# The last output feature of a two-dimensional Fourier stage: a third matmul per slice in every batch, in place of a path of its own

## The chip, the cores and the metric

The kernel runs on one core of one Trainium2 chip. The metric is the device time of one execution, in microseconds (us). A core has a matrix engine (PE, with PEld for the loading of its stationary operand), a vector engine (DVE), a scalar engine (ACT), a general engine (POOL) and a queue engine (SP) that here only issues DMA transfers. Each engine takes its instructions in the order of its own queue; they meet through semaphores.

## The reference

The input x is 8 batches of 3072 positions by 256 features. What is computed is the real part of a Fourier transform over positions and features, and on that a channel mix with a shift by one position:

```
X  = fft(fft(x, axis=1), axis=2).real
xk = mu_k * X + (1 - mu_k) * X_prev      # X_prev: one position earlier, 0 at the first
xr = mu_r * X + (1 - mu_r) * X_prev
k  = relu(xk @ w_k);  v = (k * k) @ w_v  # w_k 256x1024, w_v 1024x256
r  = sigmoid(xr @ w_r)                   # w_r 256x256
out = r * v                              # 8 x 3072 x 256, float32
```

## The kernel before

**The Fourier part of a batch.** Positions are 48 x 64. Stage A (a_item, line 391; a_sum, line 403, for inputs that have not been through the butterfly) transforms over the 48, with the weights w_pm. Stage D (d_item, line 426) transforms over features, with the table w_eo, into g_all: 24 units of 386 columns on 128 partitions, of which columns 1 to 256 hold values and the others zeros. Stage C (c_item, line 437) transforms over the 64, with the tables m1 and m2. It makes 27 slices of 64 columns, in items of 7, 7, 7 and 6 slices (in batch 0: 5, 4, 8, 8 and 2). For a slice it takes 128 columns of a unit of g_all as the stationary operand and 64 columns of a table as the moving one: columns 128 to 255 with m1 into one half of a PSUM tile, columns 0 to 127 with m2 into the other half. The ACT engine copies both halves to pq; `halves` (line 477) makes the sum and the difference of them in y, `diff` (line 484) the difference of neighbouring positions in d, and `mix` (line 518) the inputs of the channel mix.

**Feature 128.** The values of feature 128 stand in column 256 of a unit, outside the two blocks of 128 columns, and must be brought into row 0 of the second half. In batch 0 a third matmul does this: columns 256 to 383 (one column of values, 127 of zeros) with m1, added to the same PSUM columns as the second. In batches 1 to 7 it goes another way. `turned` (line 461, three DVE instructions) multiplies column 256 of all units by the table tw into u; after the last slice of the batch two matmuls with 27 columns of u as stationary operand and the table cs as moving one make a 27x64 block (line 454) in spare columns of the same PSUM tile; an ACT instruction copies it to f (line 459); `flat` (line 469) clears one element of f on DVE and sends f by a DMA on the SP queue into row 0 of y. Columns 63 and 127 of w_eo differ between the two ways: `eo_rest` (line 364) sets them for the first, and `plain_128` (line 370) changes them for the second, once, in step 5. The tables cs and tw are cut from m1 and m2 in `m_rest(0)` (line 296, instructions at lines 302 to 305 and 318) and in `plain_128` (line 376).

**The order of the work.** Up to line 629 the order is that of the code: stages A, D and C of batch 0 while the tables are still being made, with filler matmuls on zeros (keep_busy, line 138). From line 731 on there are 192 + 5 steps, 24 to a batch. Each step does one quarter of the product with w_k for a chunk of 512 positions (k_piece, line 541), then the items of matmuls that the table `work` has for this step (kind "x": stages A, D, C and the product with w_r), then a quarter of the product with w_v of five steps before (v_tile, line 566), then the DVE items of the step (kind "w"), then the output (v_out, line 577) and in odd steps the square (line 550). So stages A, D and C of a later batch stand between the products of an earlier one. `pin_order` (line 85) holds every engine to the order in which the code issues. PSUM is three tiles of 1024 columns, in turn (psW), and two of 512 (psV).

The lines of c_item that decide between the two ways:

```
for o, col, m, first, last in ((0, 128, m1, True, True), (512, 0, m2, True, b > 0),
                               (512, 256, m1, False, True))[:2 if b else 3]:
...
if b and s0 + n == NSL:
    for k in range(2):
        nc.tensor.matmul(out=ps[0:NSL, 448:512], lhsT=y_t[b, "u"][:, k],
                         rhs=cs[:, k], start=(k == 0), stop=(k == 1))
```

Of the kernel before, what the change touches and what calls it, by code (L numbers as in the profile page):

```python
# [10 lines left out]
FP16 = mybir.dt.float16  # L11
INT32 = mybir.dt.int32
UINT32 = mybir.dt.uint32
AF = mybir.ActivationFunctionType
ALU = mybir.AluOpType
# [5 lines left out]
def _v(ap, extra_offset, free_dims):  # L21
    new_ap = [list(ap.ap[0])] + [[s, c] for (s, c) in free_dims]
    return dataclasses.replace(ap, offset=ap.offset + extra_offset, ap=new_ap)
# [12 lines left out]
def kernel(  # L36
# [10 lines left out]
    nc = tc.nc  # L47
# [3 lines left out]
    P = 128  # L51
    N1, R = 48, 64
    NSL = 27
    GU = 386
    NS1 = 9

    const = ctx.enter_context(tc.tile_pool(name="const", bufs=1))
    xh_pool = ctx.enter_context(tc.tile_pool(name="xh", bufs=2))
    eo_pool = ctx.enter_context(tc.tile_pool(name="eo", bufs=2))
    y_pool = ctx.enter_context(tc.tile_pool(name="y_sb", bufs=1))  # L60
# [13 lines left out]
    def ps_w():  # L74
        return ps_slot("W", 3, 1024)
# [37 lines left out]
    V = nc.vector  # L113
# [54 lines left out]
    def phase(lo, hi):  # L168
        lo, hi = (lo + 0.5) % 1.0, (hi + 0.5) % 1.0
        if (lo, hi) not in phs:  # L170
            t = const.tile([P, 1], FP32, name=f"ph{len(phs)}")
            V.memset(t[0:64], lo * TURN)
            V.memset(t[64:128], hi * TURN)
            phs[lo, hi] = t
        return phs[lo, hi]
# [5 lines left out]
    g_all = const.tile([P, NU, GU], FP16)  # L181

    def g_zeros(u0, u1):
# [25 lines left out]
                    op0=ALU.mult, op1=ALU.add)  # L209
# [3 lines left out]
                    scalar2=1.0 / N1, op0=ALU.mult, op1=ALU.mult)  # L213
    V.tensor_tensor(out=u48, in0=u48, in1=ph48.rearrange("p a b -> p (a b)"), op=ALU.add)
    V.tensor_scalar(out=r48, in0=u48, scalar1=MAGIC, scalar2=MAGIC,
                    op0=ALU.add, op1=ALU.subtract)
# [3 lines left out]
    for g in range(2):  # L220
        for n in range(2):
            V.tensor_scalar(out=w_sg[:, n, g:g + 1], in0=hi48, scalar1=2.0 * g - 1.0,
                            scalar2=1.0 - g, op0=ALU.mult, op1=ALU.add)
        V.tensor_scalar(out=w_sg[:, 2, g:g + 1], in0=hi48, scalar1=1.0 - 2.0 * g,
                        scalar2=g - 1.0, op0=ALU.mult, op1=ALU.add)
# [5 lines left out]
                    op0=ALU.bitwise_and, op1=ALU.logical_shift_right)  # L231
    V.tensor_tensor(out=w_pm, in0=_v(t48, 0, [(0, 3), (1, 48), (0, 2)]),
                    in1=_v(w_sg, 0, [(2, 3), (0, 48), (1, 2)]), op=ALU.mult)
    V.tensor_scalar(out=pos_l, in0=pcol_i, scalar1=1, scalar2=5,
                    op0=ALU.bitwise_and, op1=ALU.logical_shift_left)
# [7 lines left out]
                    scalar2=float(TURN) / R, op0=ALU.mult, op1=ALU.mult)  # L243
# [3 lines left out]
                    scalar2=phase(0.25, 0.0), op0=ALU.mult, op1=ALU.add)  # L247
# [21 lines left out]
    m1 = const.tile([P, NSL, 64], FP16)  # L269
    m2 = const.tile([P, NSL, 64], FP16)  # L270


    tw = const.tile([P, 2, NSL], FP16)
    cs = const.tile([P, 2, 64], FP16)

    def m_angles(s0, s1):
        V.tensor_tensor(out=ang[:, s0:s1], in0=_v(ast, s0, [(1, s1 - s0), (0, 64)]),
                        in1=_v(ast, NSL, [(0, s1 - s0), (1, 64)]), op=ALU.add)
# [9 lines left out]
    lo64, hi64 = slice(0, 64), slice(64, 128)  # L288
# [7 lines left out]
    def m_rest(part):  # L296

        s = 26 if part else 0  # L300
        if not part:
            V.tensor_copy(out=cs[lo64, 0], in_=m1[lo64, 1])
            V.tensor_copy(out=cs[hi64, 0], in_=m2[hi64, 1])
            V.tensor_copy(out=cs[hi64, 1], in_=m1[hi64, 1])
            V.tensor_scalar(out=cs[lo64, 1], in0=m2[lo64, 1], scalar1=-1.0, scalar2=None,
                            op0=ALU.mult)
        if part:
            V.tensor_scalar(out=m2[hi64, 25], in0=m1[hi64, 25], scalar1=-1.0, scalar2=None,
                            op0=ALU.mult)
            V.tensor_copy(out=m1[hi64, 25], in_=m1[lo64, 25])  # L310
        for m in (m1, m2):
            V.tensor_scalar(out=m[hi64, s], in0=m[hi64, s], scalar1=-1.0, scalar2=None,
                            op0=ALU.mult)
            if part:
                V.memset(m[lo64, 25], 0.0)
            else:
                V.memset(m[hi64, 1], 0.0)
                V.tensor_copy(out=tw[:, 0 if m is m1 else 1, 0:1], in_=m[:, 0, 0:1])
                V.memset(m[:, 0, 0:1], 0.0)

    m_angles(0, NS1)
# [3 lines left out]
    w_eo = const.tile([P, 2, 128], FP16)  # L325
    V.tensor_scalar(out=pd_f, in0=pcol_f, scalar1=float(TURN) / D, scalar2=None, op0=ALU.mult)
    for c in range(2):
        V.tensor_scalar(out=ueo[:, :, c], in0=veo_i[:, :, c], scalar1=pd_f,
                        scalar2=(0.5 + 0.25 * c) * TURN, op0=ALU.mult, op1=ALU.add)
# [34 lines left out]
    def eo_rest():  # L364

        for col, sign in ((63, 0.5), (127, -0.5)):
            V.tensor_scalar(out=w_eo[:, 0, col:col + 1], in0=w_eo[:, 0, 127:128], scalar1=sign,
                            scalar2=0.5, op0=ALU.mult, op1=ALU.add)

    def plain_128():  # L370

        V.memset(w_eo[:, 0, 63:64], 1.0)
        V.tensor_scalar(out=w_eo[:, 0, 127:128], in0=w_eo[:, 0, 127:128], scalar1=-2.0,
                        scalar2=1.0, op0=ALU.mult, op1=ALU.add)
        for n, m in enumerate((m1, m2)):
            V.tensor_copy(out=tw[:, n, 1:NSL], in_=m[:, 1:NSL, 0])


    a_t = {}
    y_t = {}  # L380
# [56 lines left out]
    def c_item(b, s0, n, eng="A"):  # L437

        if s0 == 0:
            y_t[b] = y_pool.tile([P, 2, NSL, 64], FP16, name="y")  # L440
            y_t[b, "pq"] = y_pool.tile([P, 2, NSL, 64], FP16, name="pq")
        pq = y_t[b, "pq"]
        ps = ps_w()
        for i in range(n):
            sl = s0 + i
            u = {-1: 1, 24: 0, 25: 23}.get(sl - 1, sl - 1)
            for o, col, m, first, last in ((0, 128, m1, True, True), (512, 0, m2, True, b > 0),
                                           (512, 256, m1, False, True))[:2 if b else 3]:
                nc.tensor.matmul(out=ps[:, o + 64 * i:o + 64 * i + 64],  # L449
                                 lhsT=g_all[:, u, col:col + 128], rhs=m[:, sl],  # L450
                                 start=first, stop=last)
        if b and s0 + n == NSL:
            for k in range(2):
                nc.tensor.matmul(out=ps[0:NSL, 448:512], lhsT=y_t[b, "u"][:, k],
                                 rhs=cs[:, k], start=(k == 0), stop=(k == 1))
        evac(pq[:, :, s0:s0 + n, :], _v(ps, 0, [(512, 2), (64, n), (1, 64)]), eng)
        if b and s0 + n == NSL:
            y_t[b, "f"] = f = y_pool.tile([NSL, 64], FP16, name="f")
            nc.scalar.activation(out=f, in_=ps[0:NSL, 448:512], func=AF.Copy)

    def turned(b):

        y_t[b, "u"] = u = y_pool.tile([P, 2, NSL], FP16, name="u")
        for s0, n, u0, step in ((1, 24, 0, 1), (25, 2, 0, 23), (0, 1, 1, 1)):
            V.tensor_tensor(out=u[:, :, s0:s0 + n],
                            in0=_v(g_all, GU * u0 + 256, [(0, 2), (GU * step, n)]),
                            in1=tw[:, :, s0:s0 + n], op=ALU.mult)

    def flat(b):

        V.memset(y_t[b, "f"][0:1, 0:1], 0.0)
        nc.sync.dma_start(out=y_t[b][0:1, 1], in_=y_t[b, "f"])


    x_t = {}
# [159 lines left out]
    def at(step, f, *args):  # L635
        work.setdefault((step, "x" if f in (a_item, a_sum, d_item, c_item, r_item) else "w"),
                        []).append((f, args))
# [48 lines left out]
    at(14, mix, 0, 1, 1, 1)  # L686
    for n, st0 in enumerate((7, 8, 9, 10)):
        at(st0, a_item, 1, 1, n // 2, n % 2, "A")
    at(5, plain_128)
    for n, st0 in enumerate((12, 13, 13, 14, 15, 17)):  # L690
        at(st0, d_item, 1, n)
    at(18, turned, 1)
    for n, st0 in enumerate((14, 15, 18, 19)):
        at(st0, c_item, 1, (0, 7, 14, 21)[n], 7 if n < 3 else 6)

    for b in range(B):
        s0 = 24 * b

        for n, st0 in enumerate((2, 4, 6, 8) if b else ()):
            at(s0 + st0, mix, b, n // 2, 1, n % 2)  # L700
        if b + 3 < B:
            for h in range(2):
                at(s0 + 12 + 2 * h, load_xh, b + 3, h)
        t = b + 2
        if t < B:
            for n, st0 in enumerate((9, 10, 12, 14) if b else (11, 13, 15, 24)):
                at(s0 + st0, butterfly, t, n // 2, n % 2)
            for n, st0 in enumerate((18, 19, 21, 22, 23, 25, 26, 27)):
                at(s0 + st0, a_item, t, n // 4, n // 2 % 2, n % 2)
            for n, st0 in enumerate((29, 30, 31, 34, 35, 38)):  # L710
                at(s0 + st0, d_item, t, n)
            at(s0 + 39, turned, t)
            for n, st0 in enumerate((33, 37, 39, 41)):
                at(s0 + st0, c_item, t, (0, 7, 14, 21)[n], 7 if n < 3 else 6)
        t = b + 1
        if t < B:
            at(s0 + 16, halves, t, 0, 14)
            at(s0 + (18 if b else 20), halves, t, 14, 27)
            at(s0 + (19 if b else 20), diff, t, 0, 26, (0,))
            at(s0 + (18 if b else 20), flat, t)  # L720
            at(s0 + (20 if b else 22), diff, t, 0, 26, (1,))
            at(s0 + 21, mix, t, 0, 0, 0)
            at(s0 + 22, mix, t, 0, 0, 1)
            at(s0 + 24, mix, t, 1, 0, 0)
            at(s0 + 25, mix, t, 1, 0, 1)
# [51 lines left out]
```

## Time and profile before

| what | value |
|---|---|
| three runs | 461.36, 461.0 and 460.77 us; median 461.0 us |
| the profiled execution | 461.36 us; span from its first to its last instruction 459.5 us |
| PE busy | 450.2 us, 98% of the span |
| PEld, DVE, ACT, POOL busy | 329.2, 361.6, 357.9, 34.9 us |
| mean granted clock of PE | 0.998 |

The span is counted from the first instruction; the remaining 1.9 us of the execution lie around it. A timeline gives, for each engine, the start of a run of instructions, its length, line and count, and in brackets the idle time before it and what ended it. Matmuls are pipelined, so neighbouring entries on PE overlap: a matmul of 64 columns is shown with some 193 ns, but what it costs the engine is the distance from its start to the start of the next. "psW<-m,g_all" is a matmul that writes psW from m and g_all. Line 386 and line 384 are the helper that copies out of PSUM on ACT and on DVE.

### The profile page before, as it was taken

To read this page: it belongs to the slowest core of one execution; us is meant where nothing else is said; L and a number is where in the kernel's file an instruction comes from. 1 tells how busy PE (TensorE), PEld (TensorE's weight loads), DVE (VectorE), ACT (ScalarE), POOL (GpSimd) and SP (SyncE) were. 2 spreads that over 40 slices of the span, in tenths; PEclk is the share of its full clock that TensorE was granted. 3 is DMA by queue.
4 is the path that set the end of the run, shared out by engine and by line. 5 is a ranking of instruction groups with operands and counts; after the bars stand their busy time and mean duration, and the time that the engine had idled before them with its cause. 6 is when DMAs were issued, how large, how long until landed. Compare 5 with 4: busy or idle time off the path is not lost.

```text
span 459.5 us, 9810 instructions
## 1 busy us (share of the span) xinstructions
PE 450.2 (98%) x4089; PEld 329.2 (72%) x4089; DVE 361.6 (79%) x533; ACT 357.9 (78%) x397; POOL 34.9 (8%) x67
## 2 busy tenths in 40 slices
PE   8889999999999999999999999999999999999996
PEld 4657777777777777777777777777777777676765
DVE  7899978987788777978688777888679855898443
ACT  3898898788878887888878888878887888666662
POOL 8821000001000000000000000000000000000000
PEclk9999999999999999999999999999999999999999
DMA  7995462625623373324722265222222232323324
GB/s 120 147 170 100 110 137 47 139 66 119 139 47 71 56 150 95 70 58 91 165 56 65 52 138 118 69 51 66 58 60 61 56 70 47 71 59 80 70 66 95
DMA packets 32972, 40.25 MB, mean 88 GB/s; under 512 B 4480, under 2 KB 30592, under 8 KB 31584
## 3 DMA queue, kind: packets, MB, share of 16 engines
q1 hardware_dynamic: 28080, 25.07, 22.8%
q0 software_dynamic: 4688, 14.42, 18.6%
q8 instruction: 32, 0.52, 0.5%
q10 hardware_dynamic: 160, 0.13, 0.1%
q14 instruction: 12, 0.10, 0.1%
HBM read 28.84 MB, written 25.17 MB: 118 GB/s over the span
## 4 chain that ended last, share of the span: by engine, by line
PE 92%; DVE 4%; DMA 2%; issue 1%; ACT 0%; POOL 0%; SPq 0%; DVEq 0%; POOLq 0%
PE psV L573 36%; PE psW L536 35%; PE psW L559 9%; PE psW L422 4%; PE psW L398 4%; PE psW L449 3%; PE psW L412 1%; DMA xh<-in_x_dram 1%; DVE t L501 1%; DVE x L514 1%; DMA out_dram<-o 1%; DVE y L481 0%; DVE d L489 0%; DVE a L384 0%; DVE pq L384 0%
## 5 line engine op out<-in xcount | busy, mean ns | idle before, releaser
L546 ACT ACTIVATE rl<-psW 128x1024 f16<-128x1024 f32 x192 | 196.7, 1025 | 83.6 <-PE psW L536 83.6
L536 PE MATMUL psW<-x,wk 128*128 128x512 f16 (+1 forms) x776 | 197.4, 377 | 1.6 <-DVE x L514 1.3
L573 PE MATMUL psV<-wv_sb,k 128*128 128x256 f16 x1536 | 198.7, 273 | 0.0
L552 DVE TENSOR_TENSOR k<-rl 128x2048 f16<-128x2048 f16 x96 | 117.4, 1223 | 62.5 <-ACT rl L546 61.9
L573 PEld LDWEIGHTS <-k 128*128 128x128 f16 x1536 | 143.6, 98 | 20.6
L536 PEld LDWEIGHTS <-wk 128*128 128x128 f16 x776 | 75.7, 98 | 52.4 <-issue 3.1
L582 DVE SCALAR_TENSOR_TENSOR o<-psV,r 128x512 f32<-128x512 f32 (+1 forms) x97 | 66.3, 684 | 24.9 <-PE psV L573 22.4
L514 DVE TENSOR_TENSOR x<-y,t 128x1536 f16<-128x1536 f16 (+2 forms) x74 | 63.0, 851 | 2.5
L386 ACT ACTIVATE a<-psW 128x768 f16<-128x768 f32 x62 | 49.8, 807 | 4.4 <-PE psW L412 4.2
L559 PE MATMUL psW<-wr,x 128*128 128x256 f16 x384 | 49.8, 273 | 0.0
L564 ACT ACTIVATE r<-psW 128x1024 f16<-128x1024 f32 x48 | 49.0, 1021 | 0.8 <-PE psW L559 0.8
L559 PEld LDWEIGHTS <-x 128*128 128x128 f16 x384 | 37.6, 98 | 14.4 <-issue 0.2
L386 ACT ACTIVATE g_all<-psW 128x1024 f16<-128x1024 f32 (+1 forms) x47 | 47.8, 1024 | 0.0
L106 POOL DMA_DIRECT2D xh<-in_x_dram x38 | 20.0, 533 | 239.0 <-DVE eo L119 223.5
L422 PEld LDWEIGHTS <-a 128*128 128x128 f16 x384 | 25.0, 98 | 11.1 <-DVE a L384 1.0
L398 PEld LDWEIGHTS <-eo 96*128 96x128 f16 x416 | 23.4, 97 | 11.6
L119 DVE TENSOR_TENSOR eo<-xh 96x2048 f16<-96x2048 f16 x26 | 31.5, 1213 | 0.0
L422 PE MATMUL psW<-w_eo,a 128*128 128x128 f16 x376 | 28.3, 219 | 0.3 <-ACT pq L386 0.3
L386 ACT ACTIVATE pq<-psW 128x896 f16<-128x896 f32 (+5 forms) x32 | 27.6, 865 | 0.3 <-PE psW L449 0.3
L398 PE MATMUL psW<-w_pm,eo 96*128 96x96 f16 x416 | 26.3, 206 | 0.0
L449 PEld LDWEIGHTS <-g_all 128*128 128x128 f16 x459 | 17.8, 98 | 7.0 <-ACT g_all L386 0.2
L501 DVE TENSOR_SCALAR t<-d,mu_f 128x1536 f16<-128x1536 f16 (+2 forms) x42 | 22.5, 535 | 0.2
(103 smaller groups left out, 155.8 us busy)
## 6 DMA issues: line engine op xcount, KB each, us to landing
out_dram<-o SPq DMA_DIRECT2D x190, 128.0 KB, 2.4
xh<-in_x_dram POOLq DMA_DIRECT2D x28, 384.0 KB, 6.1
xh<-in_x_dram POOLq DMA_DIRECT2D x6, 192.0 KB, 6.4
wv_sb<-in_moe_w_v_dram POOLq DMA_DIRECT2D x1, 512.0 KB, 8.8
xh<-in_x_dram POOLq DMA_DIRECT2D x4, 96.0 KB, 6.9
out_dram<-o ACTq DMA_DIRECT2D x2, 64.0 KB
out_dram<-o SPq DMA_DIRECT2D x2, 64.0 KB
y<-f SPq DMA_DIRECT2D x7, 3.4 KB
```

What stands on the lines that cost most here:

```text
L386: nc.scalar.activation(out=out_ap, in_=in_ap, func=AF.Copy)
L398: nc.tensor.matmul(out=ps[:, 128 * i:128 * i + 96], lhsT=eo[:, 8 * j + i, e, :], rhs=w_pm[0:96, 0], start=True, stop=True)
L422: nc.tensor.matmul(out=_v(ps, 256 * i + 64 * (1 - e), [(128, 2), (1, 64)]), lhsT=a_t[b][:, e, 2 * u:2 * u + 2, :], rhs=w_eo[:, e, :], star ...
L449: nc.tensor.matmul(out=ps[:, o + 64 * i:o + 64 * i + 64], lhsT=g_all[:, u, col:col + 128], rhs=m[:, sl], start=first, stop=last)
L514: V.tensor_tensor(out=dst, in0=_v(y_t[b], 64 * (NSL * a + lo + 3 * m), [(1, n)]), in1=_v(x_t["t", a], 64 * lo, [(1, n)]), op=ALU.subtract ...
L536: nc.tensor.matmul(out=st["k", ds][:, 512 * hs + lo:512 * hs + hi], lhsT=wk_sb[m][a][:, 128 * fc:128 * fc + 128], rhs=xk[:, a, 512 * i + l ...
L546: nc.scalar.activation(out=st["rl"][:, 2 * ds:2 * ds + 2], in_=st["k", ds].rearrange("p (f t) -> p f t", f=2), func=AF.Relu, bias=0.0, sca ...
L552: V.tensor_tensor(out=k2_t[c][:, 2 * ds - 2:2 * ds + 2], in0=r, in1=r, op=ALU.mult)
L559: nc.tensor.matmul(out=ps[:, 256 * tb:256 * tb + 256], lhsT=x_t[b, 1, m][:, a, 512 * i + 128 * tb: 512 * i + 128 * tb + 128], rhs=wr_sb[m] ...
L564: nc.scalar.activation(out=st["r", c], in_=ps, func=AF.Sigmoid)
L573: nc.tensor.matmul(out=st["v"][:, 256 * h:256 * h + 256], lhsT=k2_t[c][:, fc, 128 * tb:128 * tb + 128], rhs=wv_sb[:, fc], start=(fc == 0), ...
L582: V.scalar_tensor_tensor(out=o.rearrange("p a b -> p (a b)")[:, 0:256 * n], in0=st["v"][:, 0:256 * n], scalar=16.0, in1=st["r", c][:, 256 ...
```

## The change

The path of its own for feature 128 goes, and all batches take the way of batch 0: a third matmul per slice. With it go the tables tw and cs and the instructions that fill them, `plain_128`, `turned`, `flat`, the two matmuls per batch and the copy to f. One DVE instruction of batch 1, the second half of `diff`, stands in step 21 in place of step 22.

```diff
-    tw = const.tile([P, 2, NSL], FP16)
-    cs = const.tile([P, 2, 64], FP16)
...
         s = 26 if part else 0
-        if not part:
-            V.tensor_copy(out=cs[lo64, 0], in_=m1[lo64, 1])
-            V.tensor_copy(out=cs[hi64, 0], in_=m2[hi64, 1])
-            V.tensor_copy(out=cs[hi64, 1], in_=m1[hi64, 1])
-            V.tensor_scalar(out=cs[lo64, 1], in0=m2[lo64, 1], scalar1=-1.0, scalar2=None,
-                            op0=ALU.mult)
...
                 V.memset(m[hi64, 1], 0.0)
-                V.tensor_copy(out=tw[:, 0 if m is m1 else 1, 0:1], in_=m[:, 0, 0:1])
                 V.memset(m[:, 0, 0:1], 0.0)
...
-    def plain_128():
-
-        V.memset(w_eo[:, 0, 63:64], 1.0)
-        V.tensor_scalar(out=w_eo[:, 0, 127:128], in0=w_eo[:, 0, 127:128], scalar1=-2.0,
-                        scalar2=1.0, op0=ALU.mult, op1=ALU.add)
-        for n, m in enumerate((m1, m2)):
-            V.tensor_copy(out=tw[:, n, 1:NSL], in_=m[:, 1:NSL, 0])
...
-            for o, col, m, first, last in ((0, 128, m1, True, True), (512, 0, m2, True, b > 0),
-                                           (512, 256, m1, False, True))[:2 if b else 3]:
+            for o, col, m, first, last in ((0, 128, m1, True, True), (512, 0, m2, True, False),
+                                           (512, 256, m1, False, True)):
...
-        if b and s0 + n == NSL:
-            for k in range(2):
-                nc.tensor.matmul(out=ps[0:NSL, 448:512], lhsT=y_t[b, "u"][:, k],
-                                 rhs=cs[:, k], start=(k == 0), stop=(k == 1))
         evac(pq[:, :, s0:s0 + n, :], _v(ps, 0, [(512, 2), (64, n), (1, 64)]), eng)
-        if b and s0 + n == NSL:
-            y_t[b, "f"] = f = y_pool.tile([NSL, 64], FP16, name="f")
-            nc.scalar.activation(out=f, in_=ps[0:NSL, 448:512], func=AF.Copy)
-
-    def turned(b):
...
-    def flat(b):
...
-    at(5, plain_128)
...
-    at(18, turned, 1)
...
-            at(s0 + 39, turned, t)
...
-            at(s0 + (18 if b else 20), flat, t)
-            at(s0 + (20 if b else 22), diff, t, 0, 26, (1,))
+            at(s0 + (20 if b else 21), diff, t, 0, 26, (1,))
```

More of the change, by code (lines that the diff above doesn't have):

```diff
@@ L451, in c_item @@
                                  start=first, stop=last)
-        if b and s0 + n == NSL:
-            for k in range(2):
-                nc.tensor.matmul(out=ps[0:NSL, 448:512], lhsT=y_t[b, "u"][:, k],
-                                 rhs=cs[:, k], start=(k == 0), stop=(k == 1))
         evac(pq[:, :, s0:s0 + n, :], _v(ps, 0, [(512, 2), (64, n), (1, 64)]), eng)
-        if b and s0 + n == NSL:
-            y_t[b, "f"] = f = y_pool.tile([NSL, 64], FP16, name="f")
-            nc.scalar.activation(out=f, in_=ps[0:NSL, 448:512], func=AF.Copy)
-    def turned(b):
[L463 to L467, printed above, removed]
-    def flat(b):
-        V.memset(y_t[b, "f"][0:1, 0:1], 0.0)
-        nc.sync.dma_start(out=y_t[b][0:1, 1], in_=y_t[b, "f"])
     x_t = {}
```

## The prediction

> **What bounds the kernel now.** I read the page's busy times and its chain first. PE is busy for 98% of the span and makes 92% of the chain that ended last; DVE makes 4%.
>
> ```profile
> PE 450.2 (98%) x4089; PEld 329.2 (72%) x4089; DVE 361.6 (79%) x533; ACT 357.9 (78%) x397; POOL 34.9 (8%) x67
> ...
> PE 92%; DVE 4%; DMA 2%; issue 1%; ACT 0%; POOL 0%; SPq 0%; DVEq 0%; POOLq 0%
> ```
>
> A share is an average, so I asked for the waits between 36 and 451 us and for busy times by stretches of one batch (54.2 us).
>
> ```profile
> ACT rl L546 <- PE psW L536: 82.8, 182, 0.7
> DVE k L552 <- ACT rl L546: 61.9, 64, 1.2
> ...
> ```
>
> ```profile
> 109.20:163.40 54.20, 54.20 (x507) 40.00 (x505) 43.30 (x54) 44.43 (x50) 2.01 (x4) 1.00 0.41 89
> ```
>
> The answer on the waits has seven rows, and in none of them does PE wait; ACT waits for PE 182 times, DVE for ACT. In the stretch, after its length, PE is busy 54.20 of 54.20 us, DVE 43.30, ACT 44.43, at a granted clock of 1.00. So from 36 us to the last products PE alone sets the pace: each nanosecond put into or taken out of its queue is one of the time, and DVE and ACT have 10 us per batch to spare. Before 34 us it is otherwise; there the chain runs over DVE.
>
> **Stage C in batches 1 to 7.** A busy matmul overlaps the next, so I take distances from start to start in the timeline of PE.
>
> ```profile
> 164.32 0.57 PE L449 MATMUL psW<-m,g_all 128*128 128x64 f16 x14
> 164.73 1.04 PE L573 MATMUL psV<-wv_sb,k 128*128 128x256 f16 x8
> ...
> 173.40 0.51 PE L449 MATMUL psW<-m,g_all 128*128 128x64 f16 x12
> 173.85 0.23 PE L454 MATMUL psW<-cs,u 128*27 128x64 f16 x2
> 174.01 1.05 PE L573 MATMUL psV<-wv_sb,k 128*128 128x256 f16 x8
> ```
>
> ```profile
> 30.28 0.86 PE L449 MATMUL psW<-m,g_all 128*128 128x64 f16 x24
> 30.97 1.03 PE L536 MATMUL psW<-x,wk 128*128 128x512 f16 x4
> ```
>
> An item of 7 slices has 14 matmuls and lasts 0.41 us (to the nanosecond, the start times say 407): 29.1 ns for a weight load and a matmul. The batch-0 item of 8 slices shows the very form that the change brings to the others, three matmuls per slice, the third adding to what the second wrote: 24 in 0.69 us, 29 ns again. The last item of a batch has 12 matmuls, which should take 12 x 29.1 = 0.35 us, but the pair of line 454 starts 0.444 us after them and lasts 0.165: the item takes 0.609 us, and the pair costs 0.26 us, not 0.06.
>
> Per batch, before: 3 x 0.407 + 0.609 = 1.83 us. After: 27 slices x 3 = 81 matmuls x 29.1 ns = 2.36 us. Difference 0.53 us; seven batches: **+3.69 us**.
>
> A rule speaks for a dearer change here. The Trainium skill, page "TensorE: Matmul & The Clock Gate", section "LDWEIGHTS (loading the stationary operand)", makes the load time proportional to the columns loaded, so that the 27-column pair would be no dearer than two common matmuls. With the pair at 2 x 29.1 ns, the change would cost 7 x 25 x 29.1 ns = 5.1 us here; the trace shows 0.26 us for the pair, and I go by it. The same page, section "Back-to-back issue gap", gives about 81 ns for a sustained pair of load and matmul at 128 columns; at that price for each of the 27 added, less the pair, the sum would be 7 x (27 x 0.081 - 0.26) = 13.5 us. The trace shows 29 ns at 64 columns.
>
> **What goes from DVE, ACT and SP in those batches.** Per batch: three DVE instructions of `turned` (0.238, 0.156 and 0.163 us) and one of 0.059, an ACT copy of 0.201 us and one DMA issue of 0.78 us on SP. All of it lies under PE, which waits for none of it, and nobody waits for f by the trace: worth 0. Were DVE the pace, it would be 0.62 us per batch. `plain_128` (0.34 us of DVE at 38.1 us) lies after PE's last start-up wait, which ends at 33.14: 0. The half of `diff` that moves up a step (1.02 us) passes one `mix` on DVE. Behind it then stand the rest of that step's `mix`, a square and an output. The next product that needs this work starts at 79.52 us, 0.1 us after the second `mix` ends; but what DVE does before that instant is the same in sum, less the 0.62 us above, so it is no later: 0. The moved step issues no DMA.
>
> **The start-up.** Here six DVE instructions go from the chain.
>
> ```profile
> 11.85 0.17 DVE L302 COPY cs<-m 64x64 f16<-64x64 f16 x1
> 12.03 0.18 DVE L303 COPY cs<-m 64x64 f16<-64x64 f16 x1
> 12.13 0.18 DVE L304 COPY cs<-m 64x64 f16<-64x64 f16 x1
> 12.33 0.17 DVE L305 TENSOR_SCALAR cs<-m 64x64 f16<-64x64 f16 x1
> ...
> 13.02 0.16 DVE L318 COPY tw<-m 128x1 f16<-128x1 f16 x1
> ...
> 13.56 0.16 DVE L318 COPY tw<-m 128x1 f16<-128x1 f16 x1
> ...
> 15.03 0.95 DVE L384 CAST a<-psW 128x768 f16<-128x768 f32 x1
> ...
> 16.15 0.55 DVE L384 CAST a<-psV 128x384 f16<-128x384 f32 x1
> ```
>
> By the start of the next instruction they take 0.67 + 0.22 + 0.20 = 1.09 us, and DVE has no gap from 11.00 to 18.7 us. The copy at 15.03 can move to 13.94 (its matmuls, the sixth group of eight, are through by then). The copy at 16.15 could move to 15.06, but its own matmuls end at 14.42 + 0.82 = 15.24: about 15.3, so a is complete at 15.85, not at 16.70. What is late next is on PE:
>
> ```profile
> 15.66 0.59 PE L142 MATMUL psV<-zeros 128*128 128x512 f16 x2 [0.42 <-ACT a L386]
> 16.75 0.62 PE L422 MATMUL psV<-w_eo,a 128*128 128x128 f16 x8 [0.49 <-DVE a L384]
> ```
>
> The two fillers wait for ACT's copy, start at 15.66 and keep PE for 2 x 0.216 us, to 16.09. Stage D then starts at 16.09 in place of 16.75: **-0.66 us**. From there on the chain is made of links that follow each other (stage D, its copies, the slices of stage C, pq on ACT, then DVE without a gap from 19.28 to 33.1), and all move together; the weights they use land by 17.6 us, the next inputs by 24.5 for 28.4. This move isn't in the trace, so I bound it: 0 if something else holds the start, and 1.09 us if all of it counts, plus 0.45 us if the multiplication at 20.34 us, 0.746 us long where three of its like take 0.30, 0.29 and 0.28, loses its delay in its new place: -1.54. I take -0.66, which comes out of the row of the fillers.
>
> **Sum.** Against the profiled execution's own time: 461.36 (span 459.5 and 1.9 around it) + 3.69 - 0.66 = 464.4 us. That execution is the slowest of three, 0.36 above their median of 461.0; from the median it is **464.0 us**, 0.66% more.
>
> **The rivals.** (a) The start-up holds back more or less than I take: at 0 the time is 461.0 + 3.69 = 464.7 us, at -1.54 it is 463.2. For a smaller gain speaks that POOL issues DMAs all through it; against it, that no wait on POOL or a DMA stands in the chain there after 6.7 us. (b) The third matmul is dearer in the steady batches than in batch 0. The dearest row of this width is the pair of line 454, 82 ns each: 7 x (27 x 0.082 - 0.26) - 0.66 = +13.0, 474.0 us. Against it: batch 0's 29 ns. (c) Not slower: the added matmuls fall into time in which PE is not working, because "busy" ends are modelled and another engine really sets the pace at each item. Then only the start-up counts: 461.0 - 0.66 = 460.3, within 0.2%, and 459.5 at the far end of the start-up. Its place is the wait on a PSUM tile ahead of each item of stage C, and it decides from 0.53 us of hidden idle time per batch upward. Against it: the starts follow each other with the same 29 ns on either side of items, and 182 waits of ACT for PE.
>
> **How the numbers follow.** My forecast with the start-up anywhere in its bounds (rival a included): 0.90, and 0.70 of it near the taken value. (b) 0.05. (c) 0.05. The range takes in both ends of the start-up, 463.2 and 464.7, with 0.2 below and 0.5 above for the spread of 0.6 us that the runs show: 463.0 to 465.2 us. About 0.2% (0.9 us) is what a measurement of this kernel can tell from no change. Slower by over 0.2%: the forecast and (b), 0.95. Within 0.2%: most of (c), 0.04. Faster: (c) with the start-up at its far end, 0.01.
>
> **What would show it.** Right: items of stage C from start to start at 0.61 us (21 matmuls) and 0.52 us (18); 175 more matmuls on PE; still no wait of PE between 36 and 451 us; stage D's first matmul near 16.1 us; the wait that ends at 33.14 ending near 32.5; a span near 462.5. The forecast falls if a stage-C item of 21 is well over 0.65 us, if PE waits appear in the steady batches, or if the 33.14 does not move earlier by 0.3 us or more, or moves by over 1.1.

## The result, and the profile after

Four runs of the changed kernel gave 463.83, 463.77, 463.74 and 463.35 us, median 463.75; the kernel before beside them 461.01. The ratio is 1.0057 (95% interval 1.0040 to 1.0075): slower by 2.74 us. The forecast was 464.0 us in a range of 463.0 to 465.2. The profiled execution took 463.83 us, its span 462.0.

The page of the changed kernel, busy times and chain:

```profile
PE 451.6 (98%) x4264; PEld 332.2 (72%) x4264; DVE 357.7 (77%) x495; ACT 357.5 (77%) x390; POOL 35.4 (8%) x67
...
PE 93%; DVE 3%; DMA 2%; POOL 0%; ACT 0%; issue 0%; SPq 0%; POOLq 0%; DVEq 0%
```

PE has 175 more matmuls (4264 against 4089), DVE 38 fewer instructions, ACT 7 fewer. The waits between 36 and 454 us again have seven rows and none of PE. Two of them (waiting engine, whom for, us in total, times, longest) and the stretch of one batch, which is now 54.7 us long:

```profile
ACT rl L507 <- PE psW L497: 86.7, 183, 0.7
DVE k L513 <- ACT rl L507: 64.3, 64, 1.2
...
```

```profile
109.60:164.31 54.71, 54.71 (x530) 40.60 (x529) 42.94 (x51) 44.35 (x48) 2.02 (x4) 1.00 0.40 88
```

PE is busy for 54.71 of 54.71 us; the batch has grown by 0.5 us, and DVE and ACT stand idle in it for 0.9 and 0.6 us longer. The items of stage C in the timeline of PE:

```profile
164.55 0.78 PE L430 MATMUL psW<-m,g_all 128*128 128x64 f16 x21
165.16 1.04 PE L534 MATMUL psV<-wv_sb,k 128*128 128x256 f16 x8
...
174.04 0.69 PE L430 MATMUL psW<-m,g_all 128*128 128x64 f16 x18
174.56 1.04 PE L534 MATMUL psV<-wv_sb,k 128*128 128x256 f16 x8
```

From start to start the item of 7 slices lasts 0.61 us, that of 6 lasts 0.52: the two figures of the forecast. Comparing the starts of the products with w_v, step by step, in both traces, the changed kernel is 0.97 us ahead at the first of them and 2.62 us behind after the last batch's stage C. So the steady batches cost 3.59 us, 0.48 in the first and 0.52 to 0.53 in each of the six others.

The start-up, DVE first, then PE:

```profile
11.53 1.36 DVE L273 TENSOR_TENSOR rl<-ast 128x1152 int32<-128x1152 f32 x1
13.50 0.96 DVE L365 CAST a<-psW 128x768 f16<-128x768 f32 x1 [0.61 <-PE psW L393]
...
15.26 0.56 DVE L365 CAST a<-psV 128x384 f16<-128x384 f32 x1 [0.55 <-PE psV L393]
```

```profile
14.40 0.82 PE L393 MATMUL psV<-w_pm,xh 96*128 96x192 f16 x8 [0.28 <-DMA xh<-in_x_dram]
15.47 0.59 PE L142 MATMUL psV<-zeros 128*128 128x512 f16 x2 [0.25 <-ACT a L367]
15.90 0.61 PE L403 MATMUL psV<-w_eo,a 128*128 128x128 f16 x8
...
32.16 1.02 PE L497 MATMUL psW<-x,wk 128*128 128x512 f16 x4 [0.51 <-DVE pq L365]
```

DVE, without the six instructions, now waits for PE ahead of both copies, and PE for the landing of the last inputs. Stage D starts at 15.90 (16.75 before), and PE's last start-up wait ends at 32.16 (33.14 before).

### The profile page after: what moved, and what is told of

Same layout as the page of the kernel before. It is cut to its first block, busy times and chain, and to the rows that moved or that the text cites. A ratio compares the mean times of both kernels' runs of the same rounds, so it can differ in the third digit from the quotient of the medians.

```text
span 462.0 us, 10095 instructions
## 1 busy us (share of the span) xinstructions
PE 451.6 (98%) x4264; PEld 332.2 (72%) x4264; DVE 357.7 (77%) x495; ACT 357.5 (77%) x390; POOL 35.4 (8%) x67
## 4 chain that ended last, share of the span: by engine, by line
PE 93%; DVE 3%; DMA 2%; POOL 0%; ACT 0%; issue 0%; SPq 0%; POOLq 0%; DVEq 0%
PE psV L534 36%; PE psW L497 35%; PE psW L520 9%; PE psW L403 4%; PE psW L379 4%; PE psW L430 4%; DMA xh<-in_x_dram 1%; PE psW L393 1%; DVE x L475 1%; DVE t L462 1%; DMA out_dram<-o 1%; DVE y L442 0%; POOL xh L106 0%; DVE d L450 0%; ACT a L367 0%
## 5 line engine op out<-in xcount | busy, mean ns | idle before, releaser
L430 PEld LDWEIGHTS <-g_all 128*128 128x128 f16 x648 | 23.3, 98 | 7.2 <-issue 0.5
L430 PE MATMUL psW<-m,g_all 128*128 128x64 f16 x648 | 24.5, 193 | 0.3 <-DVE m L290 0.2
```

The lines of the kernel that those rows point to most:

```text
L430: nc.tensor.matmul(out=ps[:, o + 64 * i:o + 64 * i + 64], lhsT=g_all[:, u, col:col + 128], rhs=m[:, sl], start=first, stop=last)
```

## The experiments

All ratios are to the kernel before, run beside each on the same chip. The runs were made in three groups, each on one chip: e1 to e4; then e9, e10, e7 and e5; then e6, e8 and e11. On the chip of the second group every kernel was some 2.4 us longer (463.41 us for the kernel before); its runs are compared among themselves. The difference lies in the start-up: in e10 the first product with w_v starts 2.35 us later than in the first profile of the same kernel, and the last ones are 2.35 us later too. In the start-up of these profiles ACT stands idle where it doesn't on the other chips. The profile puts these waits down to matmuls that the copy behind them does not read (the slices copied at 28.07 us had been through PE by 26.1 us); for what ACT waits, the traces don't say, and why this chip was slower stays open. The timeline of ACT in e10, twice 1.1 us:

```profile
17.95 0.70 ACT L367 ACTIVATE pq<-psW 128x640 f16<-128x640 f32 x1 [0.27 <-issue]
19.76 0.60 ACT L367 ACTIVATE pq<-psW 128x512 f16<-128x512 f32 x1 [1.10 <-PE psW L403]
...
28.07 1.02 ACT L367 ACTIVATE pq<-psW 128x1024 f16<-128x1024 f32 x1 [1.12 <-PE psW L403]
```

**The start-up part alone** (e1). The six instructions leave m_rest(0). The same values are taken in step 5 from entries that later code leaves alone.

```diff
-            V.tensor_copy(out=cs[lo64, 0], in_=m1[lo64, 1])
...
-                V.tensor_copy(out=tw[:, 0 if m is m1 else 1, 0:1], in_=m[:, 0, 0:1])
...
     def plain_128():
...
+        V.tensor_copy(out=tw[:, 0, 0:1], in_=m1[:, 2, 0:1])
+        V.tensor_scalar(out=tw[:, 1, 0:1], in0=m2[:, 2, 0:1], scalar1=-1.0, scalar2=None,
+                        op0=ALU.mult)
+        V.tensor_copy(out=cs[lo64, 0], in_=m1[lo64, 1])
+        V.tensor_copy(out=cs[hi64, 0], in_=m1[lo64, 1])
+        for half in (lo64, hi64):
+            V.tensor_scalar(out=cs[half, 1], in0=m2[lo64, 1], scalar1=-1.0, scalar2=None,
+                            op0=ALU.mult)
```

> The kernel before, with the six DVE instructions that fill cs and column 0 of tw moved from the start-up to step 5 (from equal entries of m1 and m2 there); feature 128 keeps its own path. My theory: the six took 1.09 us of the chain, of which 0.66 us reach the end, since the two fillers on PE are late next: 461.0 - 0.66 = 460.3 us. Rival: all of the 0.97 us by which the last start-up wait of PE ends earlier in the changed kernel (33.14 to 32.16) comes from the six: 460.0 us. Second rival: the start is held by something else and the 0.97 us are a difference between two executions: 461.0 us.

Measured 461.26 against 461.02 us, ratio 1.0002 (0.9993 to 1.0011): no gain. The first two expectations missed; the third has the number, and its reason is at most a part of it. The waits of e1 between 34 and 60 us have two rows of PE's weight loads that the kernel before does not have:

```profile
PEld L560 <- DVE x L515: 0.4, 1, 0.4
PEld L574 <- DVE k L553: 0.3, 1, 0.3
```

Against the first profile of the kernel before, the products with w_v start 0.34 us earlier in step 5 and 0.08 us later from step 10 on, so these waits cost 0.42 us. The six took 0.9 us of DVE at 38 us, where DVE is still making batch 0's inputs and has less than that to spare. How much of the 0.34 us comes from the six is not shown: against the second profile of the kernel before (e4) it is 0.08 us.

**The same with the six in step 17** (e9), where DVE has room:

```profile
65.42 1.23 DVE L552 TENSOR_TENSOR k<-rl 128x2048 f16<-128x2048 f16 x1 [1.02 <-ACT rl L546]
66.56 0.38 DVE L465 TENSOR_TENSOR u<-g_all,tw 128x48 f16<-128x48 f16 x3
68.18 0.69 DVE L582 SCALAR_TENSOR_TENSOR o<-psV,r 128x512 f32<-128x512 f32 x1 [1.23 <-PE psV L573]
```

(this is the kernel before: two waits of more than 1 us around step 18).

```diff
+    at(17, late_six)
     at(18, turned, 1)
```

> As the run with the six DVE instructions moved to step 5, but they stand in step 17, near 65 us, where DVE was idle for 1.02 and 1.23 us in the kernel before. In step 5 DVE had too little to spare: PE waited there, twice, for x and for k, and what the start had gained was gone. My theory: with that wait away the start-up gain reaches the end, 461.0 - 0.4 to 0.66 = 460.3 to 460.6 us, and no wait of PE is left between 36 and 450 us. Rival: the start is held by the landing of the last inputs, and the six are worth nothing wherever they stand: 461.0 us.

Measured 462.93 against 463.41 us, ratio 0.9987 (0.9975 to 0.9998): 0.48 us faster, and no wait of PE from 36 us on. A gain of the expected size, but the interval reaches from 0.1 to 1.2 us.

**The steady part alone** (e2): the changed kernel with the six put back where they were, filling tables that nothing reads.

```diff
         s = 26 if part else 0
+        if not part:
+            V.tensor_copy(out=cs[lo64, 0], in_=m1[lo64, 1])
...
                 V.memset(m[hi64, 1], 0.0)
+                V.tensor_copy(out=tw[:, 0 if m is m1 else 1, 0:1], in_=m[:, 0, 0:1])
```

> The changed kernel with the six DVE instructions put back at their old place (cs and tw are filled and read by nothing). My theory: only the third matmuls against the pair are left, seven batches at 0.52 us: 461.0 + 3.6 = 464.6 us. Rival: the start-up instructions cost nothing and this is the changed kernel's time, 463.75 us.

Measured 464.37 against 461.02 us, ratio 1.0074 (1.0061 to 1.0088): +3.35 us. That is nearer to the theory's 464.6 than to the rival's 463.75; by the medians the six are worth about 0.6 us in the changed kernel, but the intervals of the two ratios overlap. The products with w_v, compared as above, put the steady batches at 3.59 us again.

**The changed kernel again** (e10), and **a fourth matmul per slice** (e5), of which the stationary operand is zeros, so the sums are unchanged.

> The changed kernel once more, beside the others on the same chip. My theory: 463.75 us again (461.0 + 3.6 - 0.4 to 0.9), and PE's last start-up wait ends between 32.1 and 32.9 us. Rival: its first profile had a lucky start, and the time is 464.3 us, as with the six instructions put back.

```diff
-                                           (512, 256, m1, False, True)):
+                                           (512, 256, m1, False, b == 0),
+                                           (512, 258, m1, False, True))[:4 if b else 3]:
```

> The changed kernel with a fourth matmul per slice in batches 1 to 7, added to the same PSUM columns as the third, with 128 columns of zeros of g_all as stationary operand, so that nothing is added to the sum. My theory: each matmul of 64 columns costs 29.1 ns on PE, 7 x 27 x 29.1 ns = 5.5 us: 463.75 + 5.5 = 469.25 us. Rival: another engine sets the pace and the added ones are partly covered: under 467 us.

The changed kernel: 466.16 against 463.41 us, ratio 1.0059 (1.0046 to 1.0072), +2.75 us: the first result again, by its ratio. The expected end of PE's last start-up wait, 32.1 to 32.9 us, can't be compared on this chip, whose start-up runs otherwise. With the fourth matmul: 471.88 us, ratio 1.0182 (1.0165 to 1.0200), 5.72 us above e10. The traces of the two put it at 5.51 us over the seven batches, 189 x 29.1 ns. The timeline of e5:

```profile
168.69 0.98 PE L431 MATMUL psW<-m,g_all 128*128 128x64 f16 x28
169.50 1.04 PE L535 MATMUL psV<-wv_sb,k 128*128 128x256 f16 x8
```

28 matmuls in 0.81 us are 29 ns each, and PE waits for nothing there either. This removes rival (c): nothing covers an added matmul, not even a second one per slice.

**The pair at 128 columns** (e3): u becomes a constant tile of 128 columns, with zeros from column 27 on (UW is its width, 128 here), so the two matmuls use the whole array.

```diff
+    UW = 128
+    u_all = const.tile([P, 2, UW], FP16)
...
     def plain_128():
+        V.memset(u_all, 0.0)
...
-                nc.tensor.matmul(out=ps[0:NSL, 448:512], lhsT=y_t[b, "u"][:, k],
+                nc.tensor.matmul(out=ps[0:UW, 448:512], lhsT=u_all[:, k],
...
-        y_t[b, "u"] = u = y_pool.tile([P, 2, NSL], FP16, name="u")
+        u = u_all
```

> The kernel before, with u widened to 128 columns (the columns from 27 on are zeros, set once in step 5), so that the pair of line 454 loads and uses all 128 columns. My theory: the pair is dear, 0.26 us, because of its 27 columns; with 128 it costs 2 x 29 ns, the last stage-C item lasts 0.41 us in place of 0.61, and the time is 461.0 - 7 x 0.20 = 459.6 us. Rival: the pair waits for u or for the matmuls before it, whatever its width: no change, 461.0 us.

Measured 459.47 against 461.02 us, ratio 0.9966 (0.9954 to 0.9978): 1.55 us faster.

```profile
172.32 0.51 PE L452 MATMUL psW<-m,g_all 128*128 128x64 f16 x12
172.67 0.22 PE L457 MATMUL psW<-cs,u_all 128*128 128x64 f16 x2
172.73 1.04 PE L576 MATMUL psV<-wv_sb,k 128*128 128x256 f16 x8
```

The twelve now last 0.35 us and the pair 0.06: 0.41 us for an item that took 0.61. The pair waits for nothing; its narrowness was the price.

**64 and 32 columns** (e6), the same edit with another UW and nothing else.

> As the pair widened to 128 columns, but to 64 (columns from 27 on are zeros). My theory: what is dear is every stationary operand narrower than 128 columns, not the number 27; the item of the pair lasts 0.61 us again and the time is that of the kernel before. Rival: the cost goes with the columns or with their not being a multiple of 32, and 64 is as cheap as 128: 1.5 us less than before.

> The same with 32 columns. My theory: the item of the pair lasts 0.61 us, the time is that of the kernel before. Rival: 32 columns, a quarter of the array, are as cheap as 128: 1.5 us less than before.

Measured 461.29 us (ratio 1.0011, 1.0000 to 1.0021) and 461.11 us (1.0006, 0.9994 to 1.0017): nothing gained by either. With 64 columns:

```profile
172.34 0.51 PE L452 MATMUL psW<-m,g_all 128*128 128x64 f16 x12
172.78 0.25 PE L457 MATMUL psW<-cs,u_all 128*64 128x64 f16 x2
172.96 1.05 PE L576 MATMUL psV<-wv_sb,k 128*128 128x256 f16 x8
```

0.44 + 0.18 us, as dear as 27 columns; with 32 columns it is 0.44 + 0.165 us. Both expectations held: the price does not fall with the columns, and their divisibility by 32 does not remove it. Only 128 columns do.

**Both** (e7, and again as e11): the pair at 128 columns and the six in step 17.

> The kernel before with both: the pair widened to 128 columns and the six start-up instructions in step 17. My theory: the gains add, 461.0 - 1.5 - 0.4 to 0.66 = 458.8 to 459.1 us. Rival: the start-up part gives nothing, 459.5 us.

> The kernel before with the pair at 128 columns and the six start-up instructions in step 17, once more, since the start-up differs between executions. My theory: 1.5 + 0.5 to 0.66 = 2.0 to 2.2 us less than before. Rival: the start-up part gives nothing, 1.5 us less.

Measured 461.63 against 463.41 us, ratio 0.9952 (0.9937 to 0.9967), and on the third chip 459.7 against 460.91 us, ratio 0.9971 (0.9962 to 0.9980): 1.8 and 1.2 us (1.34 by the ratio) faster than before. This version beats the kernel before on both chips, and the changed kernel on the one where that ran beside it. The second time is less than either expectation gave, and whether the start-up part adds to the pair's 1.5 us these two runs don't agree on.

**Without the fillers** that the forecast named (e8): e9 less `keep_busy(2)` ahead of stage D.

> The kernel with the six start-up instructions in step 17, and without the two filler matmuls ahead of batch 0's first stage-D products, which my forecast named as what is late next. If they are, stage D starts up to 0.4 us earlier. Rival, which the profiles of the runs so far speak for: the copies of the last stage-A products end at the same time as the fillers, since those products wait for the landing of the last inputs near 14.5 us, and stage D starts no more than 0.1 us earlier after that landing; the time moves by less than 0.2 us.

Measured 461.03 against 460.91 us, ratio 0.9998 (0.9988 to 1.0008): nothing, neither from the fillers nor, this time, from the six.

```profile
14.73 0.82 PE L416 MATMUL psV<-w_pm,xh 96*128 96x192 f16 x8
16.29 0.61 PE L426 MATMUL psV<-w_eo,a 128*128 128x128 f16 x8 [0.74 <-DVE a L388]
```

Stage D starts 1.56 us after the start of the last stage-A products; in the changed kernel, with the fillers, 1.50. Without the fillers PE waits for DVE's copy in their place. The rival held: taking the fillers out gains nothing.

**The kernel before again** (e4).

> The kernel before once more, for its start-up. My theory: the first sixteen stage-A matmuls, 2.72 us long in the first profile and 1.48 us in that of the changed kernel, vary between executions of the same kernel, and with 1.5 us here the start-up wait of PE that ended at 33.14 ends 0.2 to 0.4 us earlier. Rival: they are 2.7 us in this kernel always, and the wait ends at 33.1 again.

Its first sixteen stage-A matmuls took 1.48 us, and the last start-up wait of PE ended at 32.87 us, 0.27 earlier than in the first profile; it took 461.11 us. The theory held: this start-up differs between executions of one kernel.

## Why the prediction was right, step by step

**The bound**: right, and tested by e5. PE alone sets the pace from 36 us on in the changed kernel too.

**The third matmul at 29.1 ns**: right. 0.61 and 0.52 us per item were forecast and found. **The steady sum**: 3.69 forecast, 3.59 in the traces. Of the 0.10 us, 0.05 lies in the first batch (0.48 and not 0.53); the rest lies in the other six, the pair having delayed the products behind it by a further 0.01 us.

**The pair at 0.26 us**: right as a row, and e3 and e6 show why. The rule of the Trainium skill (page "TensorE: Matmul & The Clock Gate", section "LDWEIGHTS (loading the stationary operand)"), by which load time goes with the columns, would have made 27 columns the cheapest of the four widths. The runs show 27, 32 and 64 alike at 0.26 to 0.28 us and 128 at 0.06; the measurement decides.

**What lies under PE**: right in value. For `plain_128` the reason was too simple: that PE has had its last start-up wait does not mean that DVE has room at 38 us. 0.9 us more there cost 0.42 (e1).

**The start-up at -0.66**: right in sign, and near in size by the times, but the stall that it was read from belongs to one execution. In the two first profiles the move was -0.97. Stage D contributed 0.85 of it (the fillers started at 15.47 and not at 15.66, because ACT's copies were earlier); a delayed multiplication (0.746 us before) took 0.29 in its new place, a copy of 0.45 took 0.70, and a multiplication of 0.30 took 0.39.

In the first profile stage D starts 0.66 us after the fillers end, because DVE's copy is late. Of the five other profiles with the six in place, on the chips without ACT's idle times, one (e2) shows 0.09 us of this, and the four others (e3, e4, both of e6) show none of it. PE in e3, with the six in place:

```profile
14.37 0.82 PE L415 MATMUL psV<-w_pm,xh 96*128 96x192 f16 x8 [0.46 <-DMA xh<-in_x_dram]
15.44 0.59 PE L142 MATMUL psV<-zeros 128*128 128x512 f16 x2 [0.25 <-ACT a L389]
15.87 0.61 PE L425 MATMUL psV<-w_eo,a 128*128 128x128 f16 x8
```

Stage D starts as the fillers end, 1.50 us after the start of the last stage-A products, as in the changed kernel. The profiles in which DVE was late are those in which the first sixteen stage-A matmuls took 2.72 us (the first one) and 2.43 us (e2); in the four others they took 1.48 us, and DVE came to the six 1 us earlier. So in these profiles the six hold stage D back only after a slow first group; that the forecast read its -0.66 in such an execution and still came out near the time is in part luck. What makes that group slow stays open. In e2, and in e8 with 2.34 us, the granted clock between 6 and 12 us was 0.72, but the first profile shows 1.00 there.

What I named as late next, the fillers, does end last ahead of stage D in the changed kernel's trace, but by 0.08 us only: the copy of 15.26 us ends at 15.82, the fillers at 15.90. Behind both stands the landing of the last inputs, which the line at 14.40 us shows, and e8 gained nothing without the fillers.

The size differs between executions by as much as the effect. The end of PE's last start-up wait in kernels with the six in place was 33.14, 32.87, 32.79, 32.48, 32.75 and 32.04 us (before twice, e2, e3, e6 at 32 and at 64), mean 32.7; without them 32.16, 32.79, 32.66 and 31.64 (the change, e1, e8, e11), mean 32.3. That is -0.4 us, with a standard deviation of 0.4 to 0.5 in either group (the chip with ACT's idle times is left out), so these profiles don't tell it from nothing. By the times: about -0.85 for the change (2.74 less 3.59), -0.6 between e2 and the change, -0.5 in e9, nothing in e8 and e11. It stays open which part of this is the six and which the execution.

**Rivals.** (b) fell with the 0.61 us; (c) with e5; the far ends of (a) were not reached.

## What to carry to other kernels

Where one engine is busy without a gap and waits for nothing, the price of an edit in its queue is the distance from start to start in its timeline, counted on both sides of the edited item; 3.69 us came out of such distances alone and 3.59 were measured. Pad a narrow stationary operand to the full width before replacing it by more matmuls: zeros in u were worth 1.5 us and the change lost 2.7. In a start-up that several landings and engines share, look at two or more executions before taking a stall at its full length, and when moving work out of it, look for idle time of that engine at the new place.

## What the runs showed of the hardware that was not expected

A matmul with a stationary operand narrower than 128 columns, between matmuls of 128, costs about 0.1 us on either side. The twelve matmuls before the pair take 0.44 and not 0.35 us to the next start. The pair takes 0.165 us at 27 and 32 columns and 0.18 at 64, and not 0.06; of this some 0.126 us stands between its second matmul and the product behind it, where 0.029 is the common step. With 128 columns both gaps are gone. Whether the load or the change of width makes them, these runs don't tell apart.
